# A two-layer pair of linear attention and MLP: the value projection of each tile replaced by sums of phi(k) times normalised rows

## The chip, the core and the metric

The kernel runs on one core of a Trainium2 chip. A core has a matrix engine (TensorE, PE in the profile; its weight loads are listed as PEld), VectorE (DVE), ScalarE (ACT), GpSimd (POOL) and SyncE (SP), which here only issues transfers (DMA). Engines run their own instruction streams and meet through semaphores. Matmuls read SBUF and write PSUM, which has eight banks of 512 fp32 columns on 128 partitions; DVE and ACT empty them. The metric is device time of one execution in microseconds (us), and the median over several runs.

## The reference

Four layers over x of 2048 tokens x 576 features: attention (A), MLP (B), attention, MLP, each on the layer norm of x and added to x. Heads are 32, of 18 features each.

```python
def _A_ref(x, wqkv, wo):
    qkv = (x @ wqkv).reshape(B, S, 3, H, Dh).transpose(2, 0, 3, 1, 4)
    q, k, v = qkv[0], qkv[1], qkv[2]
    phi = lambda t: jnp.where(t > 0, t + 1, jnp.exp(t)) + 1e-6
    pq, pk = phi(q), phi(k)
    kv = jnp.einsum("bhsd,bhse->bhde", pk, v)
    z = jnp.einsum("bhsd->bhd", pk)
    num = jnp.einsum("bhqd,bhde->bhqe", pq, kv)
    den = jnp.einsum("bhqd,bhd->bhq", pq, z)[..., None] + 1e-6
    return (num / den).transpose(0, 2, 1, 3).reshape(B, S, D) @ wo

def _B_ref(x, w1, b1, w2, b2):
    return gelu(layernorm(x) @ w1 + b1) @ w2 + b2

x = x + _A_ref(layernorm(x), ...)
x = x + _B_ref(x, ...)
x = x + _A_ref(layernorm(x), ...)
x = x + _B_ref(x, ...)
```

The sum over tokens in kv and z is linear in v, and v is the normalised row times a weight. So kv can be had from v of each token, or from the sum over tokens of phi(k) times the normalised row, multiplied by the value weight at the end.

## The kernel before

**Tiling.** Tokens go in 16 tiles of 128 (t); features in five chunks of 128 (the last has 64, padded). Heads form five groups g of 7, 7, 7, 7 and 4 heads (126 or 72 features, GR and GO). Layers are 0 (A), 1 (B), 2 (A), 3 (B).

**Normalised rows.** LNPipe takes a tile through stages at each call of `tick`: statistics on DVE (L266 to L280), rstd on POOL (L286), then the normalised row y, on DVE (L305) or POOL (L301), into one of four buffers y_ring. y is turned into yT (features on partitions), which k, v, q and the MLP read. In layer 0 tiles 0 to 5 are turned by matmuls with the identity (L329), and emptied by DVE (L332, L338) or ACT (L334, L336); tiles 6 to 15, and all tiles of the other layers, by a transposing DMA on SP's queue (L349).

**Attention, first loop (L485 to L498).** For each tile: `k_proj` (two halves of 288 columns, five matmuls each, L421; `phi_from_psum` empties each half with two activations on ACT, L367 and L372, and two operations on DVE, L374 and L378, into pk); `pre_a1` (ticks of LNPipe, in layer 0 also weight pieces and masks); `v_proj` (ten matmuls over 252 and 324 columns, L442 and L445, emptied by ACT L448 and DVE L459 into v_ring, which has a column of ones); `kv_acc` of the tile before (five matmuls, L467, into kvacc, two banks that stay open over the whole loop); from tile 4 on one `q_proj` (a group of heads by 512 tokens, five matmuls, L473). There are 20 such q, taken in order from q_left.

**Attention, behind the loop.** kvacc times a mask gives kvT (L502, L506). z is taken from the row of ones with five matmuls of one column (L512) and spread to zsel (L514, L516). `kv_wo` multiplies kvT by wo for a group (L524); `den_stage` makes denominators for 512 tokens (L539, reciprocal L547, L549); `scale_stage` spreads them (L555, ACT L557) and scales pq on DVE (L558). The second loop (L592 to L606) runs `wo_stage` per tile (ten matmuls, L566), adds the row of x on DVE (L400) and stores it to x_d in DRAM (L406), or to the output (L404).

**MLP.** `m1_group` makes four blocks of hidden features by 512 tokens (L666, emptied by ACT L662), and L713 sums over 36 blocks per tile.

**Banks and order.** PSUM pool ps_h has four banks under one tag "h" for k, q, turns, z, denominators and half of the MLP; ps_acc has two pairs, accA and accB. Inside attention and MLP `pe` chains all matmuls, so PE runs them in program order; the other engines' order is the scheduler's, held by manual dependencies where the code sets them. SP issues all transfers; `chained` keeps the order of the start-up ones: rows of x, k weights, value weights, q weights, then in `pre_a1_layer0` the late pieces (b1, wo, nine pieces of w1 with two tails each, six of w2).

Of the kernel before, what the change touches and what calls it, by code (L numbers as in the profile page):

```python
# [34 lines left out]
def build(tc, A_x, A_wqkv, A_wo, B_w1, B_b1, B_w2, B_b2, out, dbg=None, n_layers=4):  # L35
    nc = tc.nc
    dbg = dbg or {}
    with ExitStack() as ctx:
        const = ctx.enter_context(tc.tile_pool(name="const", bufs=1))
        ps_h = ctx.enter_context(tc.tile_pool(name="ps_h", bufs=4, space=PSUM))  # L40
        ps_acc = ctx.enter_context(tc.tile_pool(name="ps_acc", bufs=1, space=PSUM))
        dpool = ctx.enter_context(tc.tile_pool(name="dram", bufs=1, space=DRAM))

# [29 lines left out]
        def inner_diag(tile_, lead, n):  # L73
# [7 lines left out]
            select(maskz[:], 1.0, ALU.not_equal, -126, [[0, 7], [0, DH]], 1),  # L81
            fill(z_row, 0.0),
            select(z_row[:], 1.0, ALU.not_equal, -126, [[0, 1]], 1),
# [24 lines left out]
        NY = 4  # L108
        y_ring = [const.tile([P, DPAD], BF16, name=f"y_ring{i}") for i in range(NY)]
        NV = 2  # L110
        v_ring = [const.tile([P, G, P], BF16, name=f"v_ring{i}") for i in range(NV)]
# [12 lines left out]
        x_d = dpool.tile([NT, P, D], F32, name="x_d")  # L124

# [45 lines left out]
        load_wqkv(2)  # L171
# [6 lines left out]
        for i in (NY - 1, 0, 1, 2):  # L178
            nc.vector.memset(y_ring[i][:], 0.0)
        warm_ps = ps_h.tile([P, 512], F32, name="warm_ps", tag="h")  # L180
# [8 lines left out]
        for vr in v_ring:  # L189
            nc.gpsimd.memset(vr[:, 4, 72:126], 0.0)  # L190
            nc.gpsimd.memset(vr[:, :, 126:127], 1.0)
            nc.gpsimd.memset(vr[:, :, 127:128], 0.0)
# [28 lines left out]
        def bias_turn():  # L221
            tp = ps_h.tile([P, 8, P], BF16, name="tp", tag="h")
            pe(nc.tensor.transpose(out=tp[:, 0, 0:NF], in_=bias_stage.pop("b1")[:], identity=ident[0:NF, 0:NF]))
            cast = nc.vector.tensor_copy(out=b1T[:], in_=tp[:, 0, 0:NF])
            tc.add_manual_dep(cast.ins, dve_last["phi"], NOSYNC, reason="bias is not urgent")

        late_pieces = [piece_b1_dma, piece_wo] + [(lambda i=i: piece_w1(i)) for i in range(9)] + \
                      [(lambda i=i: piece_w2(i)) for i in range(6)]

        state = dict(ycnt=0, vcnt=0, xl=0)  # L230
# [3 lines left out]
        class LNPipe:  # L234
# [3 lines left out]
            def feed(self, xt, t, kind, norm_eng, evac_eng="dve", load_from=None, after=None, agg_after=None):  # L238
                xbar = evac_eng == "xbar"
                self.items.append(dict(stage=(0 if load_from is None else -1), xt=xt, t=t, kind=kind,  # L240
                                       norm=norm_eng, evac=evac_eng, load=load_from,
                                       after=after, xbar=xbar, agg_after=agg_after))
# [4 lines left out]
            def tick(self, transposes=1):  # L247
                for it in list(self.items):
# [44 lines left out]
                    elif st in (2, 3):  # L293
# [16 lines left out]
                        if it["kind"] == "B":  # L310
                            nc.gpsimd.tensor_copy(out=y[:, D:DPAD], in_=y[:, 4 * P:D])
                        if it["xbar"]:
# [10 lines left out]
                    elif st == 4:  # L323
                        y = it["y"]
                        t = it["t"]
                        tp = ps_h.tile([P, 8, P], BF16, name="tp", tag="h")
                        tq = ps_h.tile([P, 8, P], BF16, name="tq", tag="h") if it["evac"] == "both" else tp
# [66 lines left out]

        def residual(li, t, halves):
# [13 lines left out]
        def layer_A(li, next_kind, pre_a1=None, mid_k0=None):  # L409
            kvacc = ps_acc.tile([P, 2, 512], F32, name="kvacc", tag="accA")  # L410
            pk_tiles = {}
            v_tiles = {}
            pq = {}

            def k_proj(t, mid=None):
                tok = slice(t * P, (t + 1) * P)
                pk = blk.tile([P, D], BF16, name="pk", tag="blk")
                for half in range(2):
                    kp = ps_h.tile([P, 512], F32, name="k_ps", tag="h")
# [6 lines left out]
                    phi_from_psum(kp[:, 0:HALF], pk[:, half * HALF:(half + 1) * HALF], P, HALF,  # L426
                                  after=(dve_last["turn"] if mid is not None else None))
                pk_tiles[t] = pk

            def v_proj(t):  # L430
                tok = slice(t * P, (t + 1) * P)
                va = v_ring[state["vcnt"] % NV]
                state["vcnt"] += 1
                if t == 1 and li == 0:
                    vps = [ps_h.tile([P, 512], F32, name="v1_ps", tag="h") for _ in range(2)]
                    first, second = vps[0][:], vps[1][:]
                else:
                    vp = ps_acc.tile([P, 2, 512], F32, name="v_ps", tag="accB")
                    vps = None
                    first, second = vp[:, 0, :], vp[:, 1, :]  # L440
                for k in range(KD):
                    pe(nc.tensor.matmul(first[:, 0:252], lhsT=yT[:, k, tok], rhs=wqkv_sb[:, k, 2 * D: 2 * D + 252],  # L442
                                     start=(k == 0), stop=(k == KD - 1)))
                for k in range(KD):
                    pe(nc.tensor.matmul(second[:, 0:324], lhsT=yT[:, k, tok], rhs=wqkv_sb[:, k, 2 * D + 252: 3 * D],  # L445
                                     start=(k == 0), stop=(k == KD - 1)))
                if vps is None:
                    va_copy = nc.scalar.copy(out=va[:, 0:4, 0:126].rearrange("p (b g) c -> p b g c", b=2),  # L448
                                             in_=vp[:, :, 0:252].rearrange("p b (g c) -> p b g c", g=2))
                    if t == 0 and li == 0:  # L450
                        tc.add_manual_dep(va_copy.ins, act_last["phi"], NOSYNC, reason="keys first")
                else:
                    for b, part in enumerate((first, second)):
                        nc.scalar.copy(out=va[:, 2 * b:2 * b + 2, 0:126],
                                       in_=part[:, 0:252].rearrange("p (g c) -> p g c", g=2))
                if t == 0:
                    nc.scalar.copy(out=va[:, 4, 0:72], in_=second[:, 252:324])
                else:
                    nc.vector.tensor_copy(out=va[:, 4, 0:72], in_=second[:, 252:324])  # L459
                v_tiles[t] = va  # L460

            def kv_acc(t):
                pk = pk_tiles.pop(t)
                va = v_tiles.pop(t)
                for g in range(G):
                    dst = kvacc[:, 0, GO[g]:GO[g] + GR[g]] if g < 4 else kvacc[:, 1, 0:GR[g]]
                    pe(nc.tensor.matmul(dst, lhsT=va[:, g, :], rhs=pk[:, GO[g]:GO[g] + GR[g]],  # L467
                                     start=(t == 0 and g in (0, 4)), stop=(t == NT - 1), skip_group_check=True))

            def q_proj(g, c, defer=False):  # L470
                qp = ps_h.tile([P, 512], F32, name="q_ps", tag="h")
# [12 lines left out]
            pe_chain["on"] = True  # L484
            for t in range(NT):  # L485
                if li > 0 or t > 1:
                    k_proj(t)
                elif t == 0:
# [3 lines left out]
                pre_a1(t)  # L492
                v_proj(t)
                if t >= 1:
                    kv_acc(t - 1)
# [3 lines left out]
            kv_acc(NT - 1)  # L499
            q_proj(*q_left.pop(0))  # L500

            nc.vector.tensor_tensor(  # L502
                out=kvT[0:127, 0:4, :].rearrange("p g (h e) -> p g h e", h=7),
# [337 lines left out]
```

## Time and profile before

| | |
|---|---|
| median of 3 runs | 769.48 us (768.92 to 769.58) |
| profiled execution | 770.22 us, its span 768.5 us |
| granted TensorE clock over the span | 1.0 |
| layer 0 attention, from k of tile 1 to the MLP's first matmul | 9.34 to 106.1 us |
| layer 2 attention | 388.0 to 483.0 us |
| DVE, ACT, POOL busy in 388 to 443 us | 28.3, 40.5, 0.55 of 55 us |
| DVE, ACT, POOL busy in 443 to 483 us | 34.2, 23.9, 10.1 of 40 us |
| DMA share, 30 to 75 us | 1.02 to 1.19 in each stretch of 5 us |
| transposing DMA, issue to landing | 2.6 / 3.2 / 7.0 us (least, median, most) |

The span is the time from the first to the last recorded instruction. Matmul rows overlap: each lists a duration with its fill and drain, so the pace of a series is read from one start to the next, or from the chain of waits, where pieces lie end to end. "[0.53 <-DVE xn L400]" behind a row means that the engine stood idle for 0.53 us before it, until the DVE instruction of line 400 that writes xn was done. A row "SPq" is SP issuing a transfer.

### The profile page before, as it was taken

Reading aid. Unit: us, or ns where it says so; the run is one execution under the profiler, and the core shown is the slowest. Engines: PE = TensorE matmul, PEld = TensorE weight load, DVE = VectorE, ACT = ScalarE, POOL = GpSimd, SP = SyncE. Lnnn points to the kernel's source line nnn. Section 1 sums busy time; section 2 is a strip of 40 time slices with the busy share of each in tenths; the row PEclk is TensorE's granted clock in tenths of the full one; section 3 lists DMA queues with packets and bytes.
Section 4 is the critical chain, followed back from the end, with each engine's and each line's share of the span. In section 5 each row is a group of like instructions: output and inputs, shape, how many; then the busy total and the mean of one; then the engine's idle time right before and its main releaser. Section 6 shows DMA issues by size and latency. Waiting matters only on the chain.

```text
span 768.5 us, 15622 instructions
## 1 busy us (share of the span) xinstructions
PE 759.6 (99%) x6520; PEld 489.9 (64%) x6520; DVE 244.8 (32%) x678; ACT 329.3 (43%) x733; POOL 124.7 (16%) x205
## 2 busy tenths in 40 slices
PE   8999999999999999999999999999999999999998
PEld 5776664675477457646777766447745764674476
DVE  7876942125013402301244489362000000000000
ACT  5777546304600750263057784560065026205600
POOL 4770411013000301200100004321010010011000
PEclk9999999999999999999999999999999999999999
DMA  8799584125112502400310039774100120011010
GB/s 258 169 234 328 133 273 97 31 55 139 33 40 82 134 2 64 95 2 30 86 45 1 1 109 270 199 150 92 49 15 2 32 62 1 25 32 39 2 30 17
DMA packets 77904, 66.41 MB, mean 86 GB/s; under 512 B 44682, under 2 KB 62474, under 8 KB 77834
## 3 DMA queue, kind: packets, MB, share of 16 engines
q1 hardware_dynamic: 77834, 65.42, 32.0%
q8 instruction: 51, 0.84, 0.4%
q14 instruction: 19, 0.16, 0.1%
HBM read 39.38 MB, written 16.52 MB: 73 GB/s over the span
## 4 chain that ended last, share of the span: by engine, by line
PE 94%; DMA 2%; DVE 2%; POOL 1%; issue 0%; ACT 0%; SPq 0%; POOLq 0%; DVEq 0%
PE m_ps L713 37%; PE h_ps L666 20%; PE hp_ps L666 16%; PE wo_ps L566 5%; PE q_ps L473 5%; PE k_ps L421 4%; PE v_ps L445 2%; PE v_ps L442 2%; PE rden_ps L555 1%; DMA yT<-y_ring 1%; PE kvacc L467 1%; DMA w_sb<-in_B_w_dram 1%; DMA x<-in_A_x_dram 1%; PE den_ps L539 0%; PE kvwo_ps L524 0%
## 5 line engine op out<-in xcount | busy, mean ns | idle before, releaser
L713 PE MATMUL m_ps<-w_sb,hT 128*128 128x288 bf16 x2304 | 283.6, 286 | 0.0
L713 PEld LDWEIGHTS <-hT 128*128 128x128 bf16 x2304 | 224.5, 98 | 60.1 <-issue 3.4
L666 PEld LDWEIGHTS <-w_sb 64*128 64x128 bf16 x2304 | 124.6, 94 | 136.2 <-issue 1.9
L666 PE MATMUL hp_ps<-yT,w_sb 64*128 64x512 bf16 x1152 | 178.0, 376 | 0.0
L400 DVE TENSOR_TENSOR xn<-m_ps,x_ring 128x576 f32<-128x576 f32 (+1 forms) x32 | 24.2, 758 | 413.6 <-PE m_ps L713 413.6
L666 PE MATMUL h_ps<-yT,w_sb 64*128 64x512 bf16 x1152 | 148.0, 376 | 0.0
L671 ACT COPY relay_sb<-relay_sb 128x1 f32<-128x1 f32 x144 | 28.5, 198 | 265.2 <-PE h_ps L666 222.2
L662 ACT ACTIVATE hT<-h_ps,b1T 128x512 bf16<-128x512 f32 x144 | 91.1, 683 | 43.9 <-PE h_ps L666 43.9
L286 POOL TENSOR_TENSOR ln_rstd<-ln_u,neg_half 128x1 f32<-128x1 f32 x64 | 36.6, 572 | 356.2 <-DVE ln_u L277 227.5
L662 ACT ACTIVATE hT<-hp_ps,b1T 128x512 bf16<-128x512 f32 x144 | 91.1, 692 | 0.0
L392 POOL TENSOR_TENSOR x_ring<-x_ring,b_bc 128x576 f32<-128x576 f32 x32 | 40.7, 1275 | 242.0 <-DMA x_ring<-x_d 239.3
L666 PE MATMUL hp_ps<-yT,w_tail 64*128 64x512 bf16 x144 | 54.2, 376 | 0.0
L666 PE MATMUL h_ps<-yT,w_tail 64*128 64x512 bf16 x144 | 54.2, 376 | 0.0
L473 PE MATMUL q_ps<-yT,wqkv_sb 128*126 128x512 bf16 (+1 forms) x200 | 50.0, 382 | 0.1
L421 PE MATMUL k_ps<-wqkv_sb,yT 128*128 128x288 bf16 x320 | 44.6, 286 | 2.3 <-DMA yT<-y_ring 1.2
L566 PE MATMUL wo_ps<-kvwo,pq 126*128 126x288 bf16 (+1 forms) x320 | 43.6, 286 | 1.1 <-DVE ln_u L280 0.5
L367 ACT ACTIVATE phi_e<-k_ps 128x288 bf16<-128x288 f32 x64 | 27.0, 421 | 37.8 <-PE k_ps L421 37.7
L421 PEld LDWEIGHTS <-yT 128*128 128x128 bf16 x320 | 30.6, 98 | 14.4 <-DMA yT<-y_ring 2.2
L566 PEld LDWEIGHTS <-pq 126*128 126x128 bf16 (+1 forms) x320 | 30.4, 97 | 13.4 <-issue 1.9
L666 PEld LDWEIGHTS <-w_tail 64*128 64x128 bf16 x288 | 27.1, 94 | 17.0
L374 DVE TENSOR_SCALAR phi_e<-phi_e 128x288 bf16<-128x288 bf16 (+2 forms) x104 | 27.7, 268 | 25.4 <-ACT phi_e L367 24.9
L367 ACT ACTIVATE phi_e<-q_ps 126x512 bf16<-126x512 f32 (+1 forms) x40 | 23.9, 597 | 21.5 <-PE q_ps L473 21.2
(96 smaller groups left out, 544.7 us busy)
## 6 DMA issues: line engine op xcount, KB each, us to landing
x_ring<-x_d SPq DMA_DIRECT2D x66, 288.0 KB, 3.0
x_d<-xn SPq DMA_DIRECT2D x48, 288.0 KB, 2.6
w_sb<-in_B_w_dram SPq DMA_DIRECT2D x6, 864.0 KB, 8.7
w_sb<-in_B_w_dram SPq DMA_DIRECT2D x9, 512.0 KB, 5.1
x<-in_A_x_dram SPq DMA_DIRECT2D x16, 144.0 KB, 4.1
x_ring<-in_A_x_dram SPq DMA_DIRECT2D x16, 144.0 KB, 3.2
out_dram<-xn SPq DMA_DIRECT2D x16, 144.0 KB, 1.7
wqkv_sb<-in_A_wqkv_dram SPq DMA_DIRECT2D x3, 576.0 KB, 5.6
```

The costliest lines, as they stand in the source:

```text
L286: nc.gpsimd.tensor_tensor(out=rstd[:], in0=it["u"][:], in1=neg_half[:], op=ALU.pow)
L367: exp = nc.scalar.activation(out=e[0:rows, 0:n], in_=ps_ap, func=ACT.Exp)
L374: low = nc.vector.tensor_scalar(out=e[0:rows, 0:n], in0=e[0:rows, 0:n], scalar1=1.0, scalar2=1e-6, op0=ALU.min, op1=ALU.add)
L392: nc.gpsimd.tensor_tensor(out=xo, in0=xo, in1=b2_bc[:], op=ALU.add)
L400: total = nc.vector.tensor_tensor(out=res.rearrange("p (h n) -> p h n", h=2), in0=halves, in1=xo.rearrange("p (h n) -> p h n", h=2), op=AL ...
L421: pe(nc.tensor.matmul(kp[:, 0:HALF], lhsT=yT[:, k, tok], rhs=wqkv_sb[:, k, D + half * HALF: D + (half + 1) * HALF], start=(k == 0), stop=( ...
L473: pe(nc.tensor.matmul(qp[0:GR[g], :], lhsT=wqkv_sb[:, k, GO[g]:GO[g] + GR[g]], rhs=yT[:, k, c * CA:(c + 1) * CA], start=(k == 0), stop=(k ...
L566: pe(nc.tensor.matmul(wp[:, half, 0:HALF], lhsT=pq[(g, c)][0:GR[g], j * P:(j + 1) * P], rhs=kvwo[g][0:GR[g], half * HALF:(half + 1) * HALF ...
L662: act_last["gelu"] = nc.scalar.activation(out=hT[f][:, 0:CB], in_=dst[n], func=ACT.Gelu_apprx_tanh, bias=b1T[:, f:f + 1], scale=1.0).ins.name
L666: mm = pe(nc.tensor.matmul(dst[n], lhsT=wt, rhs=mv, start=(seen[n] == 0), stop=(seen[n] == 8)))
L671: relay = nc.scalar.copy(out=relay_sb[:, 1:2], in_=relay_sb[:, 0:1])
L713: pe(nc.tensor.matmul(acc[:, half, 0:HALF], lhsT=hT[f][:, j * P:(j + 1) * P], rhs=w2_sb[:, f, half * HALF:(half + 1) * HALF], start=(f == ...
```

## The change

`v_proj`, `kv_acc` and v_ring go. `ky_acc` takes the normalised row y of a tile itself as weights, chunk by chunk, and phi(k) (576 columns) as the moving operand, and sums a 640 x 576 matrix over the tokens in six banks: accA, accB and two single banks. A bank border can fall inside a chunk, so a chunk is cut into two matmuls. Column 576 of y is set to one, so row 64 of the last chunk is z.

In the loop the order is: first half of k of tile t, four chunks of tile t-1, second half of k, `pre_a1`, the last chunk of t-1, q. In layer 0, k of tiles 0 and 1 come first and all chunks of tile 0 follow. The pool ps_h is split into two banks under "h" and two under "g"; `bank` takes them in turn, and only "h" while the six banks are open.

Behind the loop one q, then the last tile's chunks, the copy of the six banks to SBUF (over the y buffers), two q, z from row 64, and 25 matmuls with the value weight into kv_ps, which is masked to kvT. `den_stage(0)` now stands ahead of `kv_wo(0)`. One q less is left for the second loop.

y must outlive its turn: y_ring grows to six buffers in one tile. In layer 0 `ky_acc` reads them in place. In layer 1 each y for layer 2 is stored to DRAM (y_d) and read back by `y_load`, three tiles ahead, with a memset on POOL for the column of ones.

At the start the value weights leave their place behind x of tile 2 and become the second late piece; the number of late pieces per tile changes; b1's turn moves into layer 0's second loop; layer 0's rows for the residual are loaded from tile 13 on, ahead of the last w2 pieces.

```diff
-        ps_h = ctx.enter_context(tc.tile_pool(name="ps_h", bufs=4, space=PSUM))
+        ps_h = ctx.enter_context(tc.tile_pool(name="ps_h", bufs=2, space=PSUM))
+        bank_turn = dict(n=0, both=True)
+        def bank(shape, dtype, name):
+            bank_turn["n"] += 1
+            tag = "g" if bank_turn["both"] and bank_turn["n"] % 2 == 0 else "h"
+            return ps_h.tile(shape, dtype, name=name, tag=tag)
...
-        NY = 4
...
+        NY = 6
+        y_all = const.tile([P, NY * DPAD], BF16, name="y_ring")
+        y_ring = [y_all[:, i * DPAD:(i + 1) * DPAD] for i in range(NY)]
+        ky_sb = y_all[:, 0:KD * D]
...
-        load_wqkv(2)
...
-        late_pieces = [piece_b1_dma, piece_wo] + ...
+        late_pieces = [piece_b1_dma, lambda: load_wqkv(2), piece_wo] + ...
...
+                        elif it["keep"]:
+                            nc.sync.dma_start(out=y_d[it["t"]], in_=y[:, 0:D])
+                        else:
+                            y_of[it["t"]] = y
...
+            def y_load(t):
+                y = y_ring[state["ycnt"] % NY]
+                state["ycnt"] += 1
+                nc.gpsimd.memset(y[:, D:D + 1], 1.0)
+                nc.sync.dma_start(out=y[:, 0:D], in_=y_d[t])
+                y_of[t] = y
+            def ky_acc(t, chunks):
+                if not ky:
+                    pairs = [ps_acc.tile([P, 2, 512], F32, name="ky_ps", tag=tag) for tag in ("accA", "accB")]
+                    singles = [ps_h.tile([P, 512], F32, name="ky1_ps", tag="g") for _ in range(2)]
+                    bank_turn["both"] = False
+                    ...
+                for c in chunks:
+                    d = 0
+                    while d < D:
+                        at = c * D + d
+                        n = min(D - d, 512 - at % 512)
+                        pe(nc.tensor.matmul(ky[at // 512][:, at % 512:at % 512 + n],
+                                            lhsT=y_of[t][:, c * P:(c + 1) * P], rhs=pk_tiles[t][:, d:d + n],
+                                            start=(t == 0 and at % 512 == 0), stop=(t == NT - 1),
+                                            skip_group_check=True))
+                        d += n
...
-                pre_a1(t)
-                v_proj(t)
-                if t >= 1:
-                    kv_acc(t - 1)
+                if li == 0 and t == 0:
+                    k_proj(0, mid=mid_k0)
+                    k_proj(1)
+                    pre_a1(0)
+                elif li == 0 and t == 1:
+                    pre_a1(1)
+                    ky_acc(0, range(KD))
+                else:
+                    k_proj(t, (0,))
+                    if t >= 1:
+                        ky_acc(t - 1, range(KD - 1))
+                    k_proj(t, (1,))
+                    pre_a1(t)
+                    if t >= 1:
+                        ky_acc(t - 1, (KD - 1,))
                 if t >= 4:
                     q_proj(*q_left.pop(0))
             q_proj(*q_left.pop(0))
-            kv_acc(NT - 1)
+            ky_acc(NT - 1, (KD - 1,) + tuple(range(KD - 1)))
+            nc.vector.tensor_copy(out=ky_sb[:, 2560:2880], in_=ky[5][:, 0:320])
+            nc.vector.tensor_copy(out=ky_sb[:, 2048:2560], in_=ky[4])
+            nc.scalar.copy(out=ky_sb[:, 0:1024].rearrange("p (b n) -> p b n", b=2), in_=ky_pair[0])
+            nc.vector.tensor_copy(out=ky_sb[:, 1024:2048].rearrange("p (b n) -> p b n", b=2), in_=ky_pair[1])
             q_proj(*q_left.pop(0))
+            q_proj(*q_left.pop(0))
...
+            kvp = ps_acc.tile([P, 2, 512], F32, name="kv_ps", tag="accA")
+            for c in (4, 0, 1, 2, 3):
+                rows = slice(0, 64 if c == 4 else P)
+                for g in range(G):
+                    ...
+                    pe(nc.tensor.matmul(dst, lhsT=wqkv_sb[rows, c, 2 * D + GO[g]:2 * D + GO[g] + GR[g]],
+                                        rhs=ky_sb[rows, c * D + GO[g]:c * D + GO[g] + GR[g]], ...))
...
-            kv_wo(0)
             q_proj(*q_left.pop(0))
             den_stage(0)
+            kv_wo(0)
...
-                            lnp.feed(xn, t, "A", "dve", "xbar")
+                            lnp.feed(xn, t, "A", "dve", "xbar", keep=True)
...
-                for _ in range(2 if t in (4, 7, 10) else 1):
+                for _ in range({3: 2, 5: 2, 7: 2, 10: 0, 11: 0, 12: 3, 13: 0, 14: 2}.get(t, 1)):
                     late_pieces.pop(0)()
+            if t == 13:
+                prefetch_first(0)
```

## The prediction

> **What bounds the kernel now.** I read the page's busy shares first, then the chain of waits through both attention layers, then the timelines of each engine at the spots that the change touches.
>
> ```profile
> PE 759.6 (99%) x6520; PEld 489.9 (64%) x6520; DVE 244.8 (32%) x678; ACT 329.3 (43%) x733; POOL 124.7 (16%) x205
> ```
>
> TensorE (PE) is idle for 8.9 of 768.5 us, so time falls only by PE work that goes, and any new wait of PE is paid in full. One tile of layer 2 in the chain of waits (start, us, what):
>
> ```profile
> 390.47 1.23 PE k_ps L421 x10
> 391.69 0.54 PE v_ps L442 x5
> 392.23 0.69 PE v_ps L445 x5
> 392.92 0.26 PE kvacc L467 x5
> ...
> 401.31 1.10 PE q_ps L473 x5
> ...
> 446.78 0.32 PE z_ps L512 x5
> ```
>
> The pieces lie end to end: 10 matmuls of 288 columns take 1.23 us, so a column costs 0.417 ns and a matmul some 2.7 ns more (252 columns: 107.6 ns; 324: 138 ns). Values cost 1.23 + 0.26 = 1.49 us a tile.
>
> **Work on PE.** Removed: 32 tiles x 1.49 = 47.7 us. Added: the accumulation of phi(k) times rows, 5 chunks x 576 = 2880 columns, cut at bank borders into 10 matmuls (512, 64, 448, 128, 384, 192, 320, 256, 256, 320): 1.20 + 10 x 0.0027 = 1.23 us, 32 x 1.235 = 39.5 us. Then once per layer 25 matmuls of 126 or 72 columns. Their weights are 126 wide; the nearest row is z_ps, 5 loads of that width with one column each in 0.32 us, 64 ns apiece, against 53 ns by columns: 1.33 to 1.60 us, I take 1.5, twice 3.0 us. Sum: -47.7 + 39.5 + 3.0 = **-5.2 us**. The instruction order of the two built programs agrees: 110 matmuls fewer.
>
> The short pieces (64, 128) might be bound by their weight load, whose row is 98 ns. But five kvacc matmuls, each with its own 128-wide load, took 0.26 us, so loads overlap; the 72-column one leaves at most 42 ns (260 - 4 x 55). A 64-column piece therefore costs 29 to 42 ns: at most 0.4 us over 32 tiles. The Trainium skill says more against this change: its page "TensorE: Matmul & The Clock Gate", section "LDWEIGHTS (loading the stationary operand)", puts a load at columns / 1.2, 107 ns for 128; if that bounded each piece, the 64, 128 and 192 columns would cost 78, 51 and 24 ns more, 4.9 us in all (an estimate by that page). By that rule kvacc would take 0.54 us; the trace has 0.26 and disagrees.
>
> **New waits, layer 2.** Before, a tile's phi(k) was used a whole tile (2.7 us) later. Now it is used right after the next tile's first half of k, 0.61 us, and the last chunk, 0.245 us. The timeline of layer 2's first tile:
>
> ```profile
> 387.86 1.39 PE L421 MATMUL k_ps<-wqkv_sb,yT 128*128 128x288 bf16 x10
> 389.28 0.41 ACT L367 ACTIVATE phi_e<-k_ps 128x288 bf16<-128x288 f32 x1
> 389.59 0.41 ACT L372 ACTIVATE phi_a<-k_ps 128x288 bf16<-128x288 f32 x1
> 390.27 0.31 DVE L378 TENSOR_TENSOR pk<-phi_a,phi_e 128x288 bf16<-128x288 bf16 x1
> ```
>
> The second half's matmuls end at 389.08 (10 x 0.1225 after 387.86); exp starts 0.20 later, the second activation 0.31 after that, it lasts 0.41, and the max ends at 390.58: 1.50 us. Without the statistics of tile 15 that sit between on DVE it is 0.92 + 0.06 + 0.31 + 0.05 = 1.34. The first new matmul reads columns 0 to 511, both halves, so:
> - tile 1: ready at 390.63, wanted at 389.08 + 0.61 = 389.70: 0.93.
> - tile 2: wanted 0.245 + 0.61 = 0.86 after the half, ready at 1.34: 0.48; but in DVE's new order the normalisation of tile 15 (0.58 us) stands ahead of this phi and waits for the slot that tile 0's accumulation reads until 0.245 after the half: 0.245 + 0.2 + 0.58 + 0.23 + 0.31 = 1.57, so 0.71.
> - tiles 3 and 4: 0.48 each. From tile 5 a q of 1.10 us stands between and covers it (1.96 against 1.34).
> Sum **+2.6 us**. While PE waits, nothing else runs on it; what is queued behind is late by the same.
>
> The k and q banks fall from four to two during the loop. In a full tile (0.61 + 0.98 + 0.61 + 0.245 + 1.10 = 3.55 us) the tightest reuse is the second half of k into the bank of the q before: q's two activations end 1.30 after it (0.2 + 0.5 + 0.6), wanted at 1.59. It holds, at nothing, with 0.29 less a semaphore's 0.06 to spare (lost, it would cost what it is late by, twelve times a layer); ACT loses the v casts (0.58 a tile) and has room.
>
> **New waits, layer 0.** Tiles 3, 4 and 5 are turned on PE and copied by ACT. The timeline now:
>
> ```profile
> 14.79 0.44 PE L329 MATMUL tp<-ident,y_ring 128*128 128x128 bf16 x5
> 15.29 0.41 ACT L372 ACTIVATE phi_a<-k_ps 128x288 bf16<-128x288 f32 x1
> 15.58 0.70 ACT L336 COPY yT<-tp 128x640 bf16<-128x640 bf16 x1
> 16.55 1.39 PE L421 MATMUL k_ps<-wqkv_sb,yT 128*128 128x288 bf16 x10
> ```
>
> The copy ends 1.49 after the turn begins; v and kvacc hid that. Now the next k is wanted after 0.28 (turn) + 0.245 = 0.525: wait 1.55 - 0.525 = 1.03, for tiles 3 and 4: 2.05. For tile 5 a q follows, but with two banks it waits for the second half of tile 4: 0.98 - 0.525 = 0.45. The turn of tile 2 now follows k of tile 1 (ends 10.57) and needs the row that POOL finishes at 10.89: 0.38. Sum **+2.9 us**, all before tile 5, whose k starts at 10.57 + 0.38 + 0.28 + 1.235 + 3 x 2.73 (a tile with its turn and no q) + 2 x 1.03 + 0.45 + 1.10 = 24.3, against 23.63 now.
>
> **The transposes of layer 0** (timeline of SP's queue, then of PE):
>
> ```profile
> 44.74 1.24 SPq L349 DMA_TRANSPOSE yT<-y_ring  x1
> 49.44 1.24 SPq L349 DMA_TRANSPOSE yT<-y_ring  x1
> ...
> 54.88 1.40 PE L421 MATMUL k_ps<-wqkv_sb,yT 128*128 128x288 bf16 x10 [0.36 <-DMA yT<-y_ring]
> 59.72 1.40 PE L421 MATMUL k_ps<-wqkv_sb,yT 128*128 128x288 bf16 x10 [0.87 <-DMA yT<-y_ring]
> ```
>
> From 25 us on SP issues without a pause (0.6 for a weight piece, 1.25 for its two tails, 1.24 for a transpose), so it sets when transposes start. The waits now cost 0.53 + 1.04 = 1.57 us of streaming. New order: the value weights (0.35 + 0.5) and wo now follow tile 5's work, w1's ninth piece and three w2 pieces move behind the last transposes. Tile 12's transpose still issues near 44.7 and lands 5.3 later, 50.0; its k is wanted at 49.1 (24.3, then 7 x 3.55): 0.9. Tile 13's issues some 0.7 earlier, 48.7, lands near 54.1 and is wanted at 52.7: in all 1.2 with the one before. Tiles 14 and 15 have 1.5 MB less ahead of them and land in time. So 1.2 for 1.57, **-0.35**; ends 0 (-1.57) and 3.0 (+1.4), if it lands after 7.0, the longest transpose in the trace.
>
> **After the loop.** The six banks are copied: on DVE 320, 512 and 1024 columns, by the 576-column cast (0.74) 0.47, 0.67 and 1.2 us; on ACT 1024, near 1.05. They lie under two q of 1.10 (one more than now), z and the first ten value matmuls; the last copy ends 3.7 after q number 13, its first reader comes at 4.4. Zero, up to 0.5 a layer if DVE is late. That q is taken from the wo stage, where DVE is the bound:
>
> ```profile
> 464.80 1.39 PE L566 MATMUL wo_ps<-kvwo,pq 126*128 126x288 bf16 x10 [0.53 <-DVE xn L400]
> ```
>
> PE reaches this matmul 1.08 earlier; DVE sheds one phi and an aggregate, 0.72. So 0.36 a layer, **+0.7**; 0 to 1.1.
>
> **Hidden.** In layers 1 and 2, 16 row stores and 16 loads on SP and 16 POOL memsets that wait for PE: SP waits 181 us in 29 waits for the sums that it stores, POOL is busy 0.55 of 55 us in layer 2's loop, DMA 5%. Each row store stands ahead of its transpose on SP, 0.32 us of issue, and that transpose is needed tens of us later. A reload issued when its slot frees has four tiles, 14 us, against 3.0 for x_ring<-x_d. Without that cover each late reload would cost up to 3 us.
>
> **Sum.** -5.2 + 2.6 + 2.9 - 0.35 + 0.7 = +0.7 us on the span of 768.5 (that run took 770.22, 1.7 outside the span and 0.74 above the median). On the median of 769.48: **770.2 us**, no change: less than 0.2% (1.5 us) is what a measurement of this kernel can't tell.
>
> **Rivals.**
> - *SP decides (slower).* If the extra value and wo pieces push tiles 12 and 13's transposes back instead of forward, or they take 7.0 us, the wait is 3.0 for 1.2: 772.0; with late copies after the loop 773. It decides once tile 13 lands after 54.7 us, 2.0 after it is wanted. For: SP issues without a pause, DMA share is above 1 from 30 us. Against: fewer bytes stand ahead of tiles 14 and 15.
> - *The start and the transposes give back (faster).* The value weights leave the start, x of tile 2 lands 0.54 earlier (k's wait on it now), no transpose is late (-1.2), the wo stage returns the whole q (-0.7): 767.8 or a little less. For: w2 pieces move back. Against: x of tile 2 was queued ahead of the value weights already.
> - *Short pieces bound by loads.* If every piece took the 98 ns of its load row, 64, 128 and 192 columns would cost 69, 42 and 15 ns more, 4.0 us in all: 774.2. Against: kvacc above. By the Trainium skill's load rule it would be 775.1.
> - *It doesn't do what it says* is out: the built program has no v matmul.
>
> **Chances.** Forecast 0.50 (own range 768.4 to 771.0), SP decides 0.26, loads 0.04, give-back 0.20. So faster 0.20, same 0.50, slower 0.30. The range runs from 767.0 to 772.8: the rivals' nearer parts are in, the load case and the deeper gains are out.
>
> **What would show it.** k to k in full tiles 3.55 us; ky pieces 1.23 a tile; PE waits on DVE of 0.93, 0.7, 0.5, 0.5 in layer 2; waits on ACT's yT copy near 1.0 twice in layer 0; wo_ps waiting near 0.9 on xn. It is wrong if the front waits are missing (5.5 us faster), or if a full tile takes 3.6 or more: then banks or loads bind.

## The result and the profile after

The changed kernel takes 770.73 us (median of 22 runs, 769.63 to 771.48), the kernel before 769.53 beside it: ratio 1.0016, 95% interval 1.001 to 1.0023. That is 1.2 us more, by an interval that lies above 1: a small loss, of the size that the forecast of 770.2 called no change (less than 0.2%). The profiled execution's span is 769.5 us (768.5 before).

The page's busy shares of the changed kernel:

```profile
PE 754.7 (98%) x6404; PEld 481.0 (63%) x6410; DVE 244.9 (32%) x653; ACT 315.1 (41%) x700; POOL 124.3 (16%) x214
```

PE has less to do (754.7 us busy for 759.6) and still ends 1.0 us later: its idle time grew from 8.9 to 14.8 us. Both figures are rough: this trace lacks six matmul records (6404 beside 6410 weight loads); the page of no_reload, a run below with all 6410, says 755.5. What ended those waits is in the view of waits of the changed kernel (engine, operand and line waited for; us in total, times, longest):

```profile
PE ky_ps L463 <- DVE pk L388: 1.9, 4, 0.7
PE k_ps L434 <- ACT yT L346: 1.7, 2, 0.9
PE wo_ps L592 <- DVE xn L414: 1.5, 2, 0.8
```

The first two rows did not exist before; wo_ps waited some 1.0 us there. Where they stand is in PE's timeline of the changed kernel (start, us, what, count; in brackets the idle time just before and what ended it). A group's us run to the end of its last matmul, so from the end of streaming to the next start some 0.16 us more is lost than the bracket says.

```profile
11.16 0.45 PE L339 MATMUL tp<-ident,y_ring 128*128 128x128 bf16 x5 [0.41 <-POOL y_ring L307]
...
16.43 0.79 PE L434 MATMUL k_ps<-wqkv_sb,yT 128*128 128x288 bf16 x5 [0.86 <-ACT yT L346]
...
23.37 1.24 PE L474 MATMUL q_ps<-yT,wqkv_sb 128*126 128x512 bf16 x5 [0.28 <-ACT phi_a L382]
...
46.81 0.79 PE L434 MATMUL k_ps<-wqkv_sb,yT 128*128 128x288 bf16 x5 [0.97 <-DMA yT<-y_ring]
...
51.67 1.14 PE L463 MATMUL ky_ps<-pk,y_ring 128*128 128x512 bf16 x8 [0.54 <-DVE pk L388]
...
388.67 2.00 PE L434 MATMUL k_ps<-wqkv_sb,yT 128*128 128x288 bf16 x15
391.54 1.14 PE L463 MATMUL ky_ps<-pk,y_ring 128*128 128x512 bf16 x8 [0.87 <-DVE ln_u L283]
...
394.82 1.14 PE L463 MATMUL ky_ps<-pk,y_ring 128*128 128x512 bf16 x8 [0.67 <-DVE pk L388]
...
400.69 1.14 PE L463 MATMUL ky_ps<-pk,y_ring 128*128 128x512 bf16 x8 [0.32 <-DVE pk L388]
...
403.60 0.78 PE L434 MATMUL k_ps<-wqkv_sb,yT 128*128 128x288 bf16 x5
...
407.13 0.78 PE L434 MATMUL k_ps<-wqkv_sb,yT 128*128 128x288 bf16 x5
...
465.75 1.39 PE L592 MATMUL wo_ps<-kvwo,pq 126*128 126x288 bf16 x10 [0.77 <-DVE xn L414]
```

What to see: a full tile runs at the rate that the change promises (403.60 to 407.13: 3.53 us, nothing idle; 3.81 before). All the loss is at the first tiles of both layers, at two tiles of layer 0 (46.81, 51.67) and before the fifth wo_ps. In layer 2 the four waits come to 1.03 + 0.84 + 0.49 + 0.49 = 2.85 us of streaming (10 matmuls of k and the first half of the next end at 390.51, the next matmul starts at 391.54, and so on; the third, at 397.75, is like the fourth). ACT's copy is late a second time at 20.20, by the same 0.86 and 1.03.

The view puts the first wait of layer 2 down to ln_u, which is no operand of the matmul. DVE's rows there:

```profile
391.08 0.31 DVE L388 TENSOR_TENSOR pk<-phi_a,phi_e 128x288 bf16<-128x288 bf16 x1
391.31 0.15 DVE L283 TENSOR_SCALAR ln_u<-ln_mv 128x1 f32<-128x1 f32 x1
```

pk, which the matmul does read, is done at 391.39, and ln_u, the end of a statistic that DVE runs next, at 391.46; the matmul starts at 391.54. In the three later waits PE starts some 0.05 us after pk's end. So some 0.1 us of the first wait may hang on ln_u, the rest is phi.

To find where the microsecond sits, I cut each span into three stages by PE's timeline: layer 0 from tile 1's k (9.35) to the first h_ps (106.94), layer 1 from there to layer 2's first k (388.67), layer 2 from there to its first h_ps (483.96). The same marks for every kernel of this study (us):

| kernel | layer 0 | layer 1 | layer 2 | ratio to the kernel before |
|---|---|---|---|---|
| before | 96.78 | 281.74 | 95.07 | 1 |
| changed | 97.59 | 281.73 | 95.29 | 1.0016 (1.001 to 1.0023) |
| l2_lag2 | 96.59 | 281.73 | 92.48 | 0.9981 (0.997 to 0.9992) |
| l0_turn | 96.44 | 281.74 | 95.30 | 1.0002 (0.9993 to 1.0011) |
| l0_pieces | 97.58 | 281.73 | 95.30 | 1.0014 (1.0002 to 1.0026) |
| l0_both | 97.05 | 281.73 | 95.30 | 1.0016 (1.0005 to 1.0027) |
| cut64 | 99.56 | 281.73 | 95.27 | 1.004 (1.0024 to 1.0055) |
| no_reload | 97.82 | 281.73 | 95.22 | 1.0017 (1.0006 to 1.0027) |
| both_lag2 | 97.69 | 281.73 | 92.47 | 0.9993 (0.9981 to 1.0005) |
| both_lag2_p | 96.45 | 281.74 | 92.46 | 0.9972 (0.9961 to 0.9983) |
| both_lag2_q | 94.32 | 281.73 | 93.63 | 0.9959 (0.9946 to 0.9972) |
| masks_late | 98.69 | 281.73 | 95.28 | 1.0023 (1.0011 to 1.0036) |
| wo_pool | 94.16 | 281.73 | 92.30 | 0.9946 (0.9933 to 0.996) |
| before_q | 95.13 | 281.73 | 95.08 | 0.9984 (0.9973 to 0.9994) |

Layers 1 and 2 repeat to 0.1 us from kernel to kernel wherever their code is the same, with one exception told below. Layer 0 doesn't: the changed kernel, l2_lag2 and no_reload have the same layer 0 and show 97.59, 96.59 and 97.82, because the wait on tile 11's transpose and the one for pk at tile 12 differ: 1.13 and 0.70, 0.78 and 0.1, 1.43 and 0.61 us of streaming. So a reading of layer 0 from one profile is good to about 1 us, and there the ratios decide. Of the eleven runs behind the ratio of both_lag2 four had a granted clock of 0.997 or 0.998 and took 769.5 to 770.6 us, the other seven, at 0.999 or 1.0, 767.5 to 768.7.

### The profile page after: what moved, and what is told of

Read it like the earlier page. It is cut to its first block, busy times and chain, and to the rows that moved or that the text cites. A ratio compares the mean times of both kernels' runs of the same rounds, so it can differ in the third digit from the quotient of the medians.

```text
span 769.5 us, 15406 instructions
## 1 busy us (share of the span) xinstructions
PE 754.7 (98%) x6404; PEld 481.0 (63%) x6410; DVE 244.9 (32%) x653; ACT 315.1 (41%) x700; POOL 124.3 (16%) x214
## 2 busy tenths in 40 slices
DMA packets 82514, 71.13 MB, mean 92 GB/s; under 512 B 45195, under 2 KB 67083, under 8 KB 82443
## 4 chain that ended last, share of the span: by engine, by line
PE 93%; DVE 2%; DMA 2%; ACT 1%; POOL 1%; SPq 0%; issue 0%; DVEq 0%; POOLq 0%
PE m_ps L741 37%; PE h_ps L694 20%; PE hp_ps L694 16%; PE q_ps L474 5%; PE wo_ps L592 5%; PE ky_ps L463 4%; PE k_ps L434 4%; PE rden_ps L581 1%; DMA w_tail<-in_B_w_dram 1%; DMA x<-in_A_x_dram 1%; DMA yT<-y_ring 1%; DVE rden L573 0%; ACT phi_e L377 0%; PE kv_ps L533 0%; DVE pk L388 0%
## 5 line engine op out<-in xcount | busy, mean ns | idle before, releaser
L434 PE MATMUL k_ps<-wqkv_sb,yT 128*128 128x288 bf16 x320 | 49.2, 286 | 4.1 <-ACT yT L346 1.7
L463 PE MATMUL ky_ps<-pk,y_ring 128*128 128x192 bf16 (+5 forms) x318 | 49.1, 285 | 2.8 <-DVE pk L388 1.9
L384 DVE TENSOR_SCALAR phi_e<-phi_e 128x288 bf16<-128x288 bf16 (+2 forms) x104 | 29.5, 284 | 31.6 <-ACT phi_e L377 31.2
```

The costliest lines, as they stand in the source:

```text
L384: low = nc.vector.tensor_scalar(out=e[0:rows, 0:n], in0=e[0:rows, 0:n], scalar1=1.0, scalar2=1e-6, op0=ALU.min, op1=ALU.add)
L434: pe(nc.tensor.matmul(kp[:, 0:HALF], lhsT=yT[:, k, tok], rhs=wqkv_sb[:, k, D + half * HALF: D + (half + 1) * HALF], start=(k == 0), stop=( ...
L463: pe(nc.tensor.matmul(ky[at // 512][:, at % 512:at % 512 + n], lhsT=y_of[t][:, c * P:(c + 1) * P], rhs=pk_tiles[t][:, d:d + n], start=(t = ...
```

## Experiments

### Two tiles of delay in layer 2 (l2_lag2)

```
for t in range(NT):            # li > 0 only
    k_proj(t, (0,))
    if t >= 2:
        ky_acc(t - 2, range(KD - 1))
    k_proj(t, (1,))
    if t >= 2:
        ky_acc(t - 2, (KD - 1,))
    pre_a1(t)
    ...
ky_acc(NT - 2, range(KD))      # then q, then the last tile as before
```

> In layer 2 the accumulation of phi(k) times rows runs two tiles behind k instead of one (tile t-2 in tile t); all else as in the changed kernel (770.7 us, 1.0016 of the kernel before). Theory (phi of k is used too soon): PE's four waits on pk at the front of layer 2 (1.03, 0.84, 0.49 and 0.49 us, 2.85 in all) go and no other comes: 767.9 us, ratio 0.998, with k to k in full tiles still 3.53 us. Rival (two PSUM banks pace the front, the named wait is only the last of several): k waits for its bank instead, less than 1 us is won, 770 us or more.

Measured 0.9981 (0.997 to 0.9992), median 767.69. PE's timeline of this kernel at the front of layer 2:

```profile
387.57 3.23 PE L434 MATMUL k_ps<-wqkv_sb,yT 128*128 128x288 bf16 x25
390.64 1.14 PE L463 MATMUL ky_ps<-pk,y_ring 128*128 128x512 bf16 x8
```

No bracket is left: two and a half tiles of k run through (25 matmuls), then accumulation and k alternate. Layer 2 falls from 95.29 to 92.48, 2.81 us of the 2.85 that the four waits were. From tile 2 on the number of banks is that of the changed kernel, and two of the four waits stood behind that, at tiles 3 and 4, so the banks do not pace the front. The theory holds, the rival falls.

### Layer 0: turns earlier, pieces later, both (l0_turn, l0_pieces, l0_both)

```
# l0_turn: layer 0
t == 1:    ky_acc(0, (0, 1)); pre_a1(1); ky_acc(0, (2, 3, 4))
t < 5:     k_proj(t, (0,)); ky_acc(t - 1, range(KD - 1)); pre_a1(t)
           k_proj(t, (1,)); ky_acc(t - 1, (KD - 1,))
# l0_pieces: weight pieces given out in tile t (1 where t is not named)
-{3: 2, 5: 2, 7: 2, 10: 0, 11: 0, 12: 3, 13: 0, 14: 2}
+{8: 0, 9: 0, 10: 0, 11: 0, 12: 3, 13: 0, 14: 2}
```

> In layer 0 alone the turns of tiles 3, 4 and 5 go between the first four chunks of the accumulation and the second half of k (before: behind that half), and the turn of tile 2 goes behind two chunks of tile 0's accumulation. Theory: ACT's copy gets 1.14 us of PE work as cover instead of 0.53, so the two waits of 1.03 us on ACT's yT copy, the 0.43 of the first q and most of the 0.58 of tile 2's row go, some 2.9 us: k of tile 5 starts near 21.6 instead of 24.45. But SP paces the transposes, so tile 11's still lands near 46.7 and PE waits about 4 us there instead of 1.13: 770 to 770.7 us. Rival (SP follows the rows, and the rows follow PE): transposes land as much earlier, 767.8 us.

> Weight pieces alone are moved: one a tile in tiles 2 to 7 and none in tiles 8 to 11 (before 2, 2, 2 in tiles 3, 5, 7 and 1 in tiles 8 and 9), the rest behind the last transpose of layer 0. Theory (SP's queue sets when tiles 10 to 12 land): the transpose of tile 11 issues at least 1.9 us earlier, PE's wait of 1.13 us on it goes: 769.6 us, ratio 1.0002. The wait of 0.70 us for pk at tile 12 is DVE's, and stays. Rival (POOL's row, not SP, holds the transpose): issue near 42.7 as before, 770.7 us.

> The moved turns and the moved weight pieces of the two runs before together, layer 2 as in the changed kernel. Theory (front waits and SP's queue stand one behind the other, so only both together pay): 2.9 + 1.1 us less than 770.7, 766.7 us, ratio 0.996, more than the sum of the two alone. Rival (the rows or the DMA queues still set the landing of tiles 11 to 13): 769.5 us or more, with a wait on the transpose near 3 us.

Measured 1.0002 (0.9993 to 1.0011), 1.0014 (1.0002 to 1.0026) and 1.0016 (1.0005 to 1.0027). None went as I expected. PE's timeline of l0_turn at the front, then DVE's ahead of its first wait:

```profile
17.12 1.14 PE L463 MATMUL ky_ps<-pk,y_ring 128*128 128x512 bf16 x8 [1.16 <-DVE pk L388]
```

```profile
14.56 0.45 DVE L272 BATCH_NORM_STATS2 ln_st<-x 128x6 f32<-128x288 bf16 x1
...
15.75 0.41 DVE L273 BATCH_NORM_STATS2 ln_st<-x 128x6 f32<-128x288 bf16 x1
...
16.13 0.53 DVE L384 TENSOR_SCALAR phi_e<-phi_e 128x288 bf16<-128x288 bf16 x1
...
16.76 0.31 DVE L388 TENSOR_TENSOR pk<-phi_a,phi_e 128x288 bf16<-128x288 bf16 x1
```

The waits on ACT's copy are gone, and waits of 1.16 and (at 20.76) 0.65 for pk stand in their place. The step that I moved holds the statistics of later tiles too, and on DVE these now stand ahead of phi: ACT's exp had ended at 15.45, DVE took it up at 16.13. k of tile 5 starts at 24.03 instead of 24.45, not at 21.6; counted from tile 1's k that is 0.3 us won. So my edit undid one cause and put another there: phi has as little slack as in layer 2. That the kernel was nonetheless about 1 us faster than the changed one came, beside this 0.3, from the transposes, none of which was late in its profile; a wait of 0.53 for pk (at 42.98) stands where the changed kernel has that of tile 12.

Moving the pieces took the wait on tile 11's transpose away, as the theory had it, and won nothing: in layer 0's output stage DVE's sums wait 1.29, 0.45 and 0.56 us for the store of an earlier sum, and PE for the sums (0.25 and 0.48). DVE's longest and PE's:

```profile
102.04 0.76 DVE L414 TENSOR_TENSOR xn<-wo_ps,x_ring 128x576 f32<-128x576 f32 x1 [1.29 <-DMA x_d<-xn]
...
102.85 3.92 PE L592 MATMUL wo_ps<-kvwo,pq 126*128 126x288 bf16 x30 [0.48 <-DVE xn L414]
```

SP gives out weight pieces there until 84 us, in the changed kernel until 72, and the stores of the stage land 4.3 us after their issue (median; 6.8 at most) where they took 2.9 (4.6); that the pieces make them late is likely, but no run shows it. l0_both failed with l0_turn: it has the same waits for pk (1.17 and 0.65). What these three leave open, whether SP's queue also holds back a front that is really faster, the next ones answer.

### Both layers at two tiles (both_lag2, both_lag2_p, both_lag2_q)

```
# layer 0, layer 2 as in l2_lag2
t == 1:    ky_acc(0, (0, 1)); pre_a1(1); ky_acc(0, (2, 3, 4))
t in 2..4: k_proj(t); pre_a1(t)                # both halves, then the turn
           if t < 4: ky_acc(t - 1, range(KD))
t >= 5:    k_proj(t, (0,)); ky_acc(t - 2, range(KD - 1))
           k_proj(t, (1,)); ky_acc(t - 2, (KD - 1,)); pre_a1(t)
# weight pieces: both_lag2 as in the changed kernel
# both_lag2_p: {3: 2, 5: 2, 8: 0, 10: 0, 11: 0, 12: 3, 13: 1, 14: 2}
# both_lag2_q: {5: 0, 12: 3, 14: 2}
```

> Accumulation two tiles behind k in layer 2, as in the first run; in layer 0 the tiles 2 to 4 take both halves of k, then the turn, then the accumulation of the tile before, and from tile 5 on it runs two tiles behind. Theory (layer 0's front loses by phi used too soon and by the copy's cover both, so both have to move; the front of tile 12 too): the waits of 1.03 on ACT go, three waits of 0.35 for the turn's bank and 0.3 for the first q's bank come, tile 2's row costs nothing: 1.6 us less than 3.1; no wait on pk near tile 12. With layer 2's 2.85: 766 us with the transposes as they land now, ratio 0.996; 767.5 if the transposes of tiles 10 to 13 take all of layer 0's part back. Rival (ACT is the bound of the front, 5 operations and a copy a tile): the waits come back on another operand and the time is that of the first run, 767.7 or more, ratio 0.998.

> The run before with three weight pieces (of tiles 7, 8 and 9) moved from ahead of the transposes of tiles 10 and 11 behind those of tiles 12 and 13 and the last. Theory (SP's queue sets their landing): no wait on a transpose is left in layer 0, 0.5 to 1.5 us less than the run before where that one shows such a wait, the same where it shows none. Rival (pieces pushed back crowd the residual rows of layer 0's output stage, as in the run with moved pieces, whose two waits there were 0.25 and 0.48): no gain or up to 1 us slower.

> As the run with lag two in both attention layers, with the weight pieces given out so that none stands between the transposes of tiles 8 and 9 and one at most between any two of tiles 6 to 14 (before: two there). In the two runs before, tile 9's row was ready 3.7 us before its transpose was issued, behind two pieces, and PE waited 2.54 and 1.96 us for it. Theory (SP's queue, not the rows, is what ate layer 0's gain): the transpose of tile 9 issues within 0.5 us of its row, no wait on a transpose above 0.3 us is left in layer 0, 2 us less than the run before: 765.2 us, ratio 0.9945 to 0.9955. Rival (landing takes over from issue: the transposes land 4 to 5 us after their issue whatever stands ahead): the wait moves to tiles 10 to 12 and 767 us stays.

Measured 0.9993 (0.9981 to 1.0005), 0.9972 (0.9961 to 0.9983) and 0.9959 (0.9946 to 0.9972). In both_lag2 no wait on ACT's copy or on pk is left at the front, only three of 0.35 us of streaming for the turn's bank and one of 0.33 for the first q's, as worked out; the first of the three:

```profile
13.89 0.44 PE L339 MATMUL tp<-ident,y_ring 128*128 128x128 bf16 x5 [0.19 <-ACT phi_a L382]
```

The k of tile 5 starts 12.52 us after tile 1's k, where the changed kernel has 15.10: 2.6 us earlier, 1.2 of them because tile 3's accumulation now comes after it, 1.4 won. And then, on PE:

```profile
38.71 0.79 PE L434 MATMUL k_ps<-wqkv_sb,yT 128*128 128x288 bf16 x5 [2.54 <-DMA yT<-y_ring]
```

One wait on tile 9's transpose takes it all back. SP's queue in that kernel, from the transpose of tile 8 to that of tile 9:

```profile
27.13 1.25 SPq L359 DMA_TRANSPOSE yT<-y_ring  x1
28.42 0.57 SPq L204 DMA_DIRECT2D w_sb<-in_B_w_dram  x1
...
30.98 1.26 SPq L207 DMA_DIRECT2D w_tail<-in_B_w_dram  x2
32.34 1.24 SPq L359 DMA_TRANSPOSE yT<-y_ring  x1
```

POOL finished tile 9's row at 28.67; its transpose stood behind two weight pieces until 32.34. The pieces that both_lag2_p moves (two, those of tiles 7 and 8; tile 9 keeps its one) stand behind this transpose, so it took away only the later wait (0.31 at tile 11), and 1.96 stayed at tile 9. In both_lag2_q SP's queue looks so at the same place:

```profile
24.64 1.21 SPq L359 DMA_TRANSPOSE yT<-y_ring  x1
25.89 0.59 SPq L204 DMA_DIRECT2D w_sb<-in_B_w_dram  x1
28.18 1.22 SPq L359 DMA_TRANSPOSE yT<-y_ring  x1
```

Between 26.5 and 28.2 SP waits for the row (POOL ends it at 28.16), not the row for SP; PE waits for no transpose in the layer, which falls from 97.69 to 94.32. So SP's queue and PE's front stand one behind the other in layer 0, as l0_both was meant to show, and the right pieces are those ahead of tile 9, which nothing waited for until PE came 2.6 us earlier. Two delays went together, though: in both_lag2 that transpose was issued 3.7 us after its row and landed 6.3 us after its issue, in both_lag2_q at once and 3.4. Either alone would have covered the 2.54, so the runs show that moving the pieces takes the wait away, not whether by the time that they hold SP's queue or by their bytes under way. Layer 2 of this one execution has a wait of 1.02 near its end (93.63 for 92.47), which neither of its siblings shows: DVE's sum waits 1.88 for the store of an earlier sum, as in l0_pieces.

### Is it the change or the queue? (before_q)

```
# the kernel before, pieces alone
-for _ in range(2 if t in (4, 7, 10) else 1):
+for _ in range({12: 3, 14: 2}.get(t, 1)):
```

> A control: the kernel before, with value projections and all, and its weight pieces alone given out as in the fast run with lag two (one a tile, three in tile 12, two in tile 14; before, two in tiles 4, 7 and 10). Theory (the fast run's 3 us come from the change, once its waits are out, and only the transposes' part from the queue): the 1.57 us of PE's two waits on the transposes of tiles 12 and 13 go and nothing else: 768 us, ratio 0.998. Rival (the queue alone made the gain): 766 us, ratio 0.996, the same as with the change. A ratio of 1.000 would say that these two waits are not in most executions, or come back elsewhere.

The fast run is both_lag2_q. Measured 0.9984 (0.9973 to 0.9994): layer 0 95.13 for 96.78, no wait on a transpose left, all else as it was. All twelve runs lie between 767.85 and 769.02, where the kernel before spreads from 767.93 to 771.5 beside them. That fits two waits that only some of its executions have; no second trace of it shows this. Of both_lag2_q's 0.41%, 0.16% could be had without the change. The rest, 0.25% or 1.9 us from two ratios that were not taken side by side, each good to some 0.1%, is what the change is worth in both_lag2_q. That is less than the 5 us or so that left PE: PE still waits 2.5 us there for xn (1.0 of it the odd one above) against 1.0 at the same matmuls in before_q, and 0.8 for the turns and the first q.

### Are short pieces dear? (cut64)

```
 n = min(D - d, 512 - at % 512)
+n = min(n, 64) if c == 0 else n
```

> The 512-column piece of the first chunk of each tile's accumulation is cut into eight of 64 columns, 7 matmuls more a tile and 224 in all; nothing else. Theory (a piece costs its columns and some 2.7 ns): 7 x 2.7 ns x 32 = 0.6 us more than the changed kernel's 770.7, at most 3.9 us more by the bound of 42 ns a piece; each of the 64-column pieces 29 to 42 ns apart in the trace. Rival (a short piece is bound by its weight load, 98 ns by its row): 8 x 98 - 216 ns = 0.57 us a tile, 18 us in all, 789 us.

Measured 1.004 (1.0024 to 1.0055), 1.8 us above the changed kernel by the two ratios. PE's timeline of a full tile:

```profile
404.51 0.78 PE L434 MATMUL k_ps<-wqkv_sb,yT 128*128 128x288 bf16 x5
405.12 1.16 PE L464 MATMUL ky_ps<-pk,y_ring 128*128 128x64 bf16 x15
406.12 0.78 PE L434 MATMUL k_ps<-wqkv_sb,yT 128*128 128x288 bf16 x5
...
408.06 0.78 PE L434 MATMUL k_ps<-wqkv_sb,yT 128*128 128x288 bf16 x5
```

Fifteen pieces take 1.00 us (405.12 to 406.12) where eight took 0.98, and the tile 3.55 for 3.53: 7 matmuls more cost 0.02 us, as columns plus 2.7 ns each. A 64-column matmul so takes 29 ns, though each has a load of its own (6634 matmuls and 6634 weight loads on the page). Layer 2 is not longer at all (95.27), and that has a cause of its own: four pieces of 64 columns read only the first half of phi(k), so they run before the second half is there. At the front they stand as a group of four ahead of each wait (392.37, 395.19, 398.38 and 401.21), and the waits shrink by some 0.11 us each (0.67 to 0.56, 0.33 and 0.32 to 0.21), which pays for the 0.3 that the pieces cost. The rise is in layer 0 (99.56), where the wait on tile 11's transpose is 2.17 in place of 0.97 and two waits for pk of 0.41 and 0.21 stand; the pieces themselves make 0.3 there (7 x 2.7 ns x 16). The rival of the loads falls: it would have shown 18 us. With it falls, for this width, the bound that the prediction weighed. By the Trainium skill's page "TensorE: Matmul & The Clock Gate", section "LDWEIGHTS (loading the stationary operand)", columns / 1.2, a load of 128 columns takes 107 ns; a matmul with a load of its own took 29 here.

### Do the stores and reloads of rows cost? (no_reload)

```
-nc.sync.dma_start(out=y[:, 0:D], in_=y_d[t])                # y_load
-nc.sync.dma_start(out=y_d[it["t"]], in_=y[:, 0:D])          # keep
```

> Layers 1 and 2 without the 16 stores of normalised rows to memory and the 16 loads of them; layer 2 accumulates with whatever rows its ring holds, so that part of the computation is left out. Theory (this traffic lies wholly beside PE's work): as the changed kernel, 770.7 us, ratio 1.0016, with the same four waits on pk at the front of layer 2. Rival (the stores on SP delay transposes or sums, or the loads the rows): 1 to 3 us faster, 768 to 769.7.

Measured 1.0017 (1.0006 to 1.0027), the ratio of the changed kernel, and layer 2 95.22 for 95.29. The traffic (66.40 MB for 71.13) is hidden.

### What slows phi at tile 12? (masks_late)

```
-if t >= 4:
+if t >= 13:
     masks(2)
```

> The changed kernel with the mask steps of POOL given out from tile 13 on, not from tile 4 on. Theory (DVE's phi operations take two to three times as long while POOL runs, and phi has no slack left to hide it): in tiles 10 to 12 the two phi operations of 0.64 to 0.98 us are back to 0.23 and 0.31 where POOL is idle, and the wait on pk at tile 12 (0.54 to 0.70) is gone; 0.5 us less at tile 12, and up to as much back after tile 13, where the masks then run: 770 to 770.7 us. Rival (the phi operations are long for what ACT or DVE itself does): same long operations, same wait.

DVE and POOL of the changed kernel just before the wait at 51.67, first DVE, then POOL:

```profile
49.67 0.86 DVE L384 TENSOR_SCALAR phi_e<-phi_e 128x288 bf16<-128x288 bf16 x1 [0.85 <-ACT phi_e L377]
50.63 0.98 DVE L388 TENSOR_TENSOR pk<-phi_a,phi_e 128x288 bf16<-128x288 bf16 x1
```

```profile
48.64 0.87 POOL L307 TENSOR_SCALAR y_ring<-x,ln_rstd,ln_nmr 128x576 bf16<-128x576 bf16 x1
49.47 2.01 POOL L74 TENSOR_SCALAR_AFFINE_SELECT head_bc<-head_bc 128x630 bf16<-128x630 bf16 x2
```

The two operations take 0.86 and 0.98 us while POOL makes two masks of about 1.0 each, and each ends within 0.15 us of the end of one mask. In masks_late, at the same tile, with POOL idle from 48.72 to 51.67, DVE:

```profile
49.70 0.23 DVE L384 TENSOR_SCALAR phi_e<-phi_e 128x288 bf16<-128x288 bf16 x1 [0.49 <-ACT phi_e L377]
50.04 0.31 DVE L388 TENSOR_TENSOR pk<-phi_a,phi_e 128x288 bf16<-128x288 bf16 x1
```

Now they take 0.23 and 0.31. The wait at tile 12 is gone, and one of 1.24 us on pk stands at tile 14 (59.45), beside the masks that now run there. In this execution the price moved and rose; ratio 1.0023 (1.0011 to 1.0036), no gain. That these two operations are held by POOL's is shown. Not every operation beside POOL is: at 41.42 in the changed kernel the first of the two takes 0.24 us beside a POOL row listed from 41.24 to 42.18. The Trainium skill's page "SBUF — State Buffer", section "SBUF: two separate sides", says that DVE, in a two-port mode or with two inputs in SBUF, and GpSimd share one pair of ports as an exclusive lock for the whole instruction. The rows at tile 12 agree with it for the second operation, which has two inputs in SBUF; in what mode the first runs, no run here shows.

### Is DVE the bound of the output stage? (wo_pool)

```
-nc.vector.tensor_tensor(out=pq[(g, c)][0:GR[g], 0:CA], ...
+(nc.gpsimd if g == 3 and c == 1 else nc.vector).tensor_tensor(out=pq[(g, c)][0:GR[g], 0:CA], ...
```

> The first run of this call with one of DVE's five scalings (group 3 of the second chunk, 0.36 us) in each output stage given to POOL. Theory (DVE is the bound of the output stage's front): the wait of 0.93 us on xn before the fifth wo_ps falls to near 0.55, 0.7 us less over two layers, ratio 0.001 below that run. Rival (POOL's operation slows DVE's while it runs, as in the loop): no gain, the wait stays at 0.9 or more.

The first run of this call is both_lag2_q. PE's fourth and fifth wo_ps of layer 2:

```profile
457.45 1.39 PE L613 MATMUL wo_ps<-kvwo,pq 126*128 126x288 bf16 x10
459.36 1.48 PE L613 MATMUL wo_ps<-kvwo,pq 126*128 126x288 bf16 x10 [0.51 <-DVE ln_u L286]
```

The fifth, which came 0.93 us after the end of the fourth, now comes 0.67 after it (457.45 + 1.24 to 459.36), short of the 0.55 expected, but with one operation less DVE is ready sooner, so DVE is the bound. But POOL's operation takes 1.56 us, some DVE rows beside it are longer (0.58 for 0.37), and of the 0.26 only 0.17 reaches the end of the stage (layer 2 92.30 for the 92.47 of both_lag2). Ratio 0.9946 (0.9933 to 0.996), 764.99 us: the fastest kernel here, though its interval overlaps that of both_lag2_q, so the gain of this one step is not told apart. Both lie clear of the kernel before and of the changed one.

## Why the prediction came out

- *Work on PE, -5.2.* The pieces were right: full tile 3.53 for 3.55, the 25 matmuls of kv_ps 1.56 (447.19 to 448.75) for 1.5. The pages say -4.9, and -4.1 with no matmul record missing, but they count some 0.16 us of tail at each new wait as work. Clean of that is l2_lag2, whose layer 2 has no wait on phi: it is 2.59 us shorter than before, with 0.32 lost in the output stage (below), so PE's work fell by 2.9 there. The forecast has 2.6 a layer. Part of the rest is q, which takes 1.08 us in a full tile now and took 1.10 behind kvacc; why, no run shows.
- *Layer 2's front, +2.6.* 2.85, and taking the cause away gave 2.81 back. The mechanism and the order of the four waits were right; tiles 1 and 2 were 0.10 and 0.13 short.
- *Layer 0's front, +2.9.* 0.58 + 1.03 + 1.03 + 0.43 = 3.07; the two 1.03 were met to the hundredth. Mended together (both_lag2) these waits shrink to 1.4 in all; that gain stays hidden until SP's queue is mended too.
- *Transposes, -0.35 (1.2 left).* The forecast's own figures for tile 13, landing at 54.1 and wanted at 52.7, give 1.4, not 1.2. The profile shows 1.13, but at tile 11, not 12 and 13, and other executions of the same layer 0 show 0.78 or 1.4. I had looked at the tiles that were late before, with SP's times kept; the tile that is late is the one whose transpose stands behind two pieces when PE arrives.
- *After the loop, 0.* No late copy. Right.
- *Output stage, +0.36 a layer.* From the first wo_ps to h_ps layer 2 takes 26.95 for 27.71, 0.76 back of the q's 1.08: +0.32. Layer 0 takes 27.18 for 27.71, with 0.2 of b1's turn moved into it. Right.
- *Not in the sum:* the wait at tile 12, 0.70 us of streaming. My cover for a full tile (1.96 against 1.34) took DVE's rows at their undisturbed length; next to POOL's masks they need up to 1.3 us more, and 1.34 + 1.30 against 1.96 is 0.68 late. With the 0.25 and 0.17 by which the two fronts were short it makes 1.1 us that the sum lacked. It hardly shows (+1.0 in the profile for +0.7) because PE's work fell by some 0.3 a layer more than forecast, in layer 0 by the same reckoning.
- *Rivals.* "SP decides" named a real mechanism, with its point too late: it did not decide in the changed kernel, but as soon as the front was mended it did, at tile 9. "Give back" did not come: k of tile 1 starts at 9.35 us (9.34 before), and the output stages kept 0.3 each. Loads and traffic are out by cut64 and no_reload.

The mechanism held, but that the sum hit so closely is partly luck: the DVE wait was missed and made up for by work that had been put too low, and what layer 0's transposes cost is a matter of 1 us from one execution to the next.

## What to carry on

A step that shortens the bound engine also shortens the time that its neighbours had: here each product was taken up one tile later before and half a tile later after, and one more tile of delay, at no cost in work, gave 2.8 us back in a layer. Where two queues stand behind one another, mending the first shows nothing until the second is mended too; look whose product is ready and not fetched (a row finished 3.7 us before its transpose was issued). And give a cover some slack in the measured length of the operations when another engine disturbs them, not their best length.

## What I had not expected of the hardware

- DVE's two bf16 operations of phi stretch from 0.23 and 0.31 to 0.86 and 0.98 us beside the masks of POOL, each to about the end of one mask.
- A 64-column matmul with a 128-wide weight load of its own runs in 29 ns, in a row of nine.
- One and the same order of layer 0 took 96.59, 97.59 and 97.82 us, by when a transpose landed and whether phi then met a mask of POOL, while layers 1 and 2 repeated to 0.1 us, but for one execution in which a store of a sum was late.
